# Routed attention and a PReLU feed-forward: the staging loads of the row orderings handed out two scatters later

## The chip, the core and the metric

The kernel runs on one core of a Trainium2 chip. Its engines are TensorE (PE, with weight loads PEld), VectorE (DVE), ScalarE (ACT), GpSimd (POOL) and the queue engine SyncE (SP). The metric is device time in microseconds of one execution. A profile records one execution and takes times from the start of its span.

## The reference

Attention in which a query sees only the keys of its own cluster, then a feed-forward layer with a PReLU. The sizes are 4 batches, 8 heads, 768 tokens, 64 values a head, 16 clusters a head; the layer has 3072 rows, 512 inputs and 2048 hidden values. All in float32.

```python
q_assign = np.argmax(np.einsum('bhsd,hcd->bhsc', q_n, c_n), axis=-1)   # nearest centroid
k_assign = np.argmax(np.einsum('bhsd,hcd->bhsc', k_n, c_n), axis=-1)
mask = q_assign[:, :, :, None] == k_assign[:, :, None, :]
scores = np.where(mask, scale * np.matmul(q, k.transpose(0, 1, 3, 2)), -1000000000.0)
attn = softmax(scores)                                                 # row by row
x = np.matmul(attn, v)              # (B,H,S,D) -> (B*S, H*D)
h = x @ w_in
out = (np.maximum(h, 0.0) + alpha * np.minimum(h, 0.0)) @ w_out
```

## The kernel before, in words

**Pairs and steps.** Two heads of one batch make a pair, numbered 0 to 15. Pairs 0 to 8 compute all scores and mask them. Pairs 9 to 15, seven in all, are first *ordered*: their tokens are sorted by cluster, so that tokens of one cluster lie side by side and only a band of scores need be computed. The program is one long list of steps. A step has five slots; in each slot the host code that writes the program calls pieces of work (`tick`, `prepare`, `feed`) and so fixes the order of the instructions on every engine. Each engine takes its own instructions strictly in that order and waits for others by semaphores. Pieces of the feed-forward layer (L1066, L1084) are fed between the attention's matmuls, so that TensorE always has work.

**One ordering.** `order_rows` (L615) finishes the target row of each token. The rows of q, k and v are then sent through SBUF into a scratch tensor in DRAM in sorted order:

- `order_stage(n, i)` (L654), six loads per ordering, i = 0 to 5. A load is three transfers on SP's queue (q, k and v, L661) into one of two staging buffers, `stage[i % 2]`.
- `order_scatter(n, i, x)` (L666), four scatters per load. Each is one indirect transfer on POOL (L675) that writes 128 rows of the buffer to their places. Before the first of the four, POOL copies the token numbers into the buffer (L672). In front of each slot that has scatters, `pace` (L648) makes POOL wait for a token from ACT, so that scatters spread over time.

The text calls load 2 of ordering 12 "12.2" and its scatters "scatter 12.2". Load i may write its buffer when the four scatters of load i - 2 have landed.

**The list of pieces.** `order_rows` appends all this to the deque `sorting` (L627 to L632), as pairs of a count and a piece: a scatter counts one, a load nothing. In the slots the main loop (L1580 to L1585) takes pieces while there is room; `scatters_at` (L1421) gives 0, 1 or 2 scatters a slot.

**What follows an ordering on SP's queue.** `order_load(n)` (L681), 12 transfers (L688, L697, L706), fetches the sorted rows of pair n from scratch, three or four steps before that pair's scores. DVE transposes them in `order_blocks` (L710, L713). After the pair's attention, `put_back` (L1008) scatters the result rows to their original order with 12 indirect transfers on POOL (L1011), `fetch_back` (L1016) reads them on SP (L1023), and DVE's `turn_back` (L1030) puts them into the layer's input. On the same SP queue are `load` and `load_v` (q, k, v of later pairs, L127 and L141), copies of the weights `w_in_kept` (L1114) and the output stores (L1095, after the `y` of L1092).

Of the kernel before, what the change touches and what calls it, by code (L numbers as in the profile page):

```python
# [23 lines left out]
def kernel(  # L24
# [70 lines left out]
    def later(slots, piece):  # L95
        due.setdefault(now[0] + slots, []).append(piece)
# [277 lines left out]
    NX = GT * NG  # L374
# [114 lines left out]
    PARTS = 3  # L489
    STAGES = 2  # L490
    us, ranks, orders, scratch, sorts = {}, {}, {}, {}, {}
    sorting = deque()
# [112 lines left out]
    def order_ranks(n, ps):  # L605
        member, count = us.pop(n)
        ordp, order = sorts["ordp"], sorts["order"]
        begin = ordp.tile([P, 2], FP32, name="begin")
        nc.vector.tensor_tensor(out=begin, in0=ps[:, 0:2], in1=sorts["shift"], op=ALU.add)
        nc.vector.tensor_copy(out=sorts["begins"][:, n - NO:n - NO + 1], in_=ps[:, 0:1])  # L610
        nc.vector.scalar_tensor_tensor(out=count, in0=count, scalar=begin[:, 1:2],
                                       in1=member, op0=ALU.add, op1=ALU.mult)
        later(1, lambda: order_rows(n, begin, count))

    def order_rows(n, begin, count):  # L615
        ordp, order = sorts["ordp"], sorts["order"]
        by_token = ordp.tile([P, NX, 2, NC], FP32, name="by_token")
        nc.vector.transpose(out=by_token.rearrange("p x h c -> p (x h c)"), in_=count)
        rank = ordp.tile([P, NX, 2], FP32, name="rank")
        nc.vector.tensor_reduce(out=rank, in_=by_token, axis=AX.X, op=ALU.add)  # L620
        off = order.tile([P, NX, 2], I32, name="off")
        nc.vector.tensor_scalar(out=off, in0=rank, scalar1=0.0, scalar2=float(2 * S - 1),
                                op0=ALU.max, op1=ALU.min)
        ranks[n] = off
        whole = tc.dram_tile([2 * 2 * S, P], FP32, name=f"scratch{n}")
        scratch[n] = whole, dram_disjoint_views(whole, 2 * NX)
        for i in range(2 * PARTS + STAGES):  # L627
            if i >= STAGES:
                for x in range(NX // PARTS):
                    sorting.append((1, lambda i=i - STAGES, x=x: order_scatter(n, i, x)))  # L630
            if i < 2 * PARTS:
                sorting.append((0, lambda i=i: order_stage(n, i)))  # L632
        later(2, lambda: order_clusters(n, begin))

    def order_clusters(n, begin):
        ordp, order = sorts["ordp"], sorts["order"]

        begun = ordp.tile([P, HS], BF16, name="mine")
        nc.vector.tensor_scalar(out=begun, in0=sorts["place"], scalar1=begin[:, 0:1],
                                scalar2=None, op0=ALU.is_ge)  # L640
        begunT = asg.tile([P, 2 * NX, NC], BF16, name="top")
        nc.vector.transpose(out=begunT.rearrange("p t c -> p (t c)"), in_=begun)
        first = order.tile([P, 2 * NX], BF16, name="cluster")
        with nc.allow_low_precision(reason="integers up to 16"):
            nc.vector.tensor_reduce(out=first, in_=begunT, axis=AX.X, op=ALU.add)
        firsts[n] = first
# [7 lines left out]
    def order_stage(n, i):  # L654

        b, hp = pairs[n]
        h, part = divmod(i, PARTS)
        head, t = 2 * hp + h, sorts["stage"][i % STAGES]
        rows = slice(part * S // PARTS, (part + 1) * S // PARTS)
        for src, p0, d0 in ((q, 0, 0), (k, TS, 0), (v, TS, D)):  # L660
            nc.sync.dma_start(out=t[p0:p0 + TS, :, d0:d0 + D],  # L661
                              in_=src[b, head, rows].rearrange("(x p) d -> p x d", p=TS))
# [3 lines left out]
    def order_scatter(n, i, x):  # L666
        scattered.setdefault(n, []).append((i, x))
        h, part = divmod(i, PARTS)
        m = NX // PARTS
        xx = part * m + x  # L670
        if x == 0:
            nc.gpsimd.tensor_copy(  # L672
                out=sorts["stage"][i % STAGES].bitcast(I32)[0:TS, :, D],
                in_=sorts["number"][0:TS, part * m:(part + 1) * m])
        nc.gpsimd.indirect_dma_start(  # L675
            out=scratch[n][1][h * NX + xx],
            out_offset=bass.IndirectOffsetOnAxis(ap=ranks[n][:, xx, h:h + 1], axis=0),
            in_=sorts["stage"][i % STAGES][:, x, :], in_offset=None,
            element_offset=h * 2 * S * P)
# [781 lines left out]
    for u in range(-AHEAD, TOGETHER):  # L1461
        for piece in load_at.get(u, []):
            piece()
        n, half, s = steps[max(u, 0)]
# [51 lines left out]
    for u in range(TOGETHER, NS + 1):  # L1516
        for piece in load_at.get(u, []):
            piece()
        if u < NS:
            n, half, s = steps[u]  # L1520
# [50 lines left out]
        for i in slots:  # L1571
# [10 lines left out]
            while sorting and room:  # L1582
                scatters, piece = sorting.popleft()
# [234 lines left out]
```

## Time and profile before

| | us |
|---|---|
| median of 3 runs (951.78 to 957.11) | 953.47 |
| the profiled execution, whole | 932.13 |
| its span, first to last instruction | 930.4 |
| TensorE busy in it | 916.0 |
| VectorE busy | 654.3 |
| GpSimd busy | 389.1 |
| ScalarE busy | 262.2 |

The profile's page gives the busy time of each engine, then the span in forty equal slices (a digit is the busy share in tenths), then the chain of work that ended last, then the costliest groups of instructions. Two more views are used below. The view of waits lists, for one engine, the instruction that stood, what ended its wait, the total time, how often, and the longest. The timeline lists instructions with their start and length, and in brackets the idle time of the engine just before and what ended it. The trace has 168 scatters (L675, mean 1079 ns), 42 loads (126 transfers of 64 KB) and 84 put-backs (L1011, mean 1018 ns). By stretches of the span, TensorE was busy as follows:

| stretch, us | what runs | TensorE busy, us | GpSimd busy, us |
|---|---|---|---|
| 0 to 75 | start, weights arrive | 69.30 | 25.79 |
| 75 to 278 | pairs without an ordering | 202.75 | 32.77 |
| 278 to 477 | orderings 9 to 13, beside pairs without one | 197.57 | 142.21 |
| 477 to 645 | ordered pairs, orderings 13 to 15 beside them | 166.34 | 122.19 |
| 645 to 780 | last ordered pairs | 135.00 | 66.12 |
| 780 to 930 | last part of the layer | 144.99 | 0.00 |

### The profile page before, as it was taken

How to read it: one execution, taken by the hardware profiler on the slowest of the kernel's cores; microseconds unless marked ns; L12 is line 12 of the kernel's file. 1: busy time of each engine (PE TensorE's matmuls, PEld its weight loads, DVE VectorE, ACT ScalarE, POOL GpSimd, SP SyncE). 2: the span in 40 equal slices, each digit the busy share in tenths (PEclk: the TensorE clock that was granted, in tenths of full speed). 3: DMA queues.
4: the chain of work that ended last, by engine and by line, in shares of the span. 5: the costliest groups of instructions: out<-in, count | busy, mean ns of one | idle time of the engine just before them, and what ended most of it. 6: DMA issues, size and time to landing. Idle time of an engine off the chain costs nothing.

```text
span 930.4 us, 11983 instructions
## 1 busy us (share of the span) xinstructions
PE 916.0 (98%) x3963; PEld 494.6 (53%) x3963; DVE 654.3 (70%) x1246; ACT 262.2 (28%) x660; POOL 389.1 (42%) x579
## 2 busy tenths in 40 slices
PE   8999999999999999999999999999999999999997
PEld 5534444445445454455555554555555555556886
DVE  5797788889769699598997899764647135598200
ACT  5764454223123122232222332122222121221000
POOL 2433232200006768587766787677723470000000
PEclk9999999999999999999999999999999999999999
DMA  8433659028001625453762283643511012000000
GB/s 301 132 123 93 148 128 159 18 56 179 26 1 51 153 73 145 88 107 85 156 133 42 50 136 96 142 87 95 97 37 27 12 38 54 1 0 1 23 23 26
DMA packets 226708, 77.71 MB, mean 84 GB/s; under 512 B 210752, under 2 KB 214544, under 8 KB 226640
## 3 DMA queue, kind: packets, MB, share of 16 engines
q1 hardware_dynamic: 217728, 62.72, 30.6%
q0 software_dynamic: 8064, 13.78, 4.7%
q8 instruction: 33, 0.54, 0.3%
q10 hardware_dynamic: 848, 0.39, 0.2%
q14 instruction: 35, 0.29, 0.1%
HBM read 52.25 MB, written 24.25 MB: 82 GB/s over the span
## 4 chain that ended last, share of the span: by engine, by line
PE 94%; DVE 4%; issue 1%; POOL 0%; ACT 0%; DVEq 0%; ACTq 0%; POOLq 0%
PE fps L1066 27%; PE fps L1084 27%; PE sps L784 7%; PE vps L939 7%; PE sps L1302 4%; PE sps L1246 4%; PE fps L784 3%; PE vps L1246 2%; PE vps L1302 2%; PE vps L972 1%; PE mps L972 1%; PE fps L1302 1%; PE fps L1246 1%; PE sps L793 1%; PE mps L894 1%
## 5 line engine op out<-in xcount | busy, mean ns | idle before, releaser
L1066 PE MATMUL fps<-xT,w_in_sb 128*128 128x384 f32 x768 | 259.3, 491 | 0.0
L1084 PE MATMUL fps<-w_out_sb,gT 128*128 128x512 f32 x576 | 254.1, 595 | 0.3 <-DVE gT L1058 0.3
L675 POOL DMA_INDIRECT scratch<-stage,off x168 | 181.3, 1079 | 67.1 <-DMA stage<-in_v_dram 29.5
L1066 PEld LDWEIGHTS fps<-xT,w_in_sb 128*128 128x128 f32 x768 | 142.3, 190 | 103.2 <-issue 4.9
L1084 PEld LDWEIGHTS fps<-w_out_sb,gT 128*128 128x128 f32 x576 | 107.5, 190 | 132.2 <-issue 122.6
L1072 ACT COPY gT<-fps 128x384 f32<-128x384 f32 x96 | 46.0, 479 | 235.9 <-PE fps L1066 235.9
L652 POOL COPY paced<-pace 1x1 f32<-1x1 f32 x204 | 55.0, 270 | 135.7 <-ACT pace L651 135.2
L1058 DVE SCALAR_TENSOR_TENSOR gT<-gT,alpha 128x384 f32<-128x384 f32 x96 | 61.5, 648 | 60.8 <-ACT gT L1072 60.7
L1011 POOL DMA_INDIRECT back<-rows,off x84 | 85.6, 1018 | 22.2 <-issue 16.5
L784 PE MATMUL sps<-qkT 64*128 64x384 f32 (+1 forms) x464 | 85.0, 485 | 0.0
L805 ACT ACTIVATE E<-sps 128x768 f32<-128x768 f32 (+1 forms) x76 | 56.3, 786 | 62.1 <-PE sps L793 39.7
L784 PEld LDWEIGHTS sps<-qkT 64*128 64x128 f32 x464 | 41.2, 186 | 38.6 <-issue 15.5
L825 DVE SCALAR_TENSOR_TENSOR more<-aq,key,more 128x384 f32<-128x384 bf16 (+2 forms) x116 | 60.4, 579 | 0.0
L939 PE MATMUL vps<-E,vt 128*64 128x384 f32 x292 | 54.2, 495 | 1.5 <-DVE xT L1042 1.5
L271 POOL TENSOR_TENSOR w_in_sb<-w_in_sb,power 128x512 f32<-128x512 f32 x16 | 26.9, 1684 | 67.4 <-DVE w_in_sb L268 67.4
L271 POOL TENSOR_TENSOR w_out_sb<-w_out_sb,power 128x512 f32<-128x512 f32 x16 | 22.5, 1411 | 56.0 <-DVE w_out_sb L268 56.0
L825 DVE SCALAR_TENSOR_TENSOR E<-aq,key,E 128x384 f32<-128x384 bf16 (+2 forms) x88 | 45.0, 569 | 0.6 <-ACT E L802 0.6
L835 DVE TENSOR_TENSOR acc<-acc,E 128x768 f32<-128x768 f32 x35 | 33.3, 951 | 14.5 <-ACT E L805 13.6
L907 DVE RECIPROCAL inverses<-mps 64x12 f32<-64x12 f32 (+1 forms) x42 | 10.5, 249 | 45.7 <-PE mps L894 39.8
L1090 ACT COPY y<-fps 128x512 f32<-128x512 f32 x18 | 10.6, 587 | 99.2 <-PE fps L1084 99.2
L1092 DVE TENSOR_TENSOR y<-y,fps 128x512 f32<-128x512 f32 x24 | 16.4, 682 | 27.6 <-PE fps L1084 27.6
L805 ACT ACTIVATE more<-sps 128x768 f32<-128x768 f32 (+1 forms) x40 | 29.2, 764 | 12.2 <-PE sps L784 11.8
(284 smaller groups left out, 1174.1 us busy)
## 6 DMA issues: line engine op xcount, KB each, us to landing
raw<-in_moe_w_in_dram SPq DMA_DIRECT2D x16, 512.0 KB, 5.2
raw<-in_moe_w_out_dram SPq DMA_DIRECT2D x16, 512.0 KB, 4.3
out_dram<-y SPq DMA_DIRECT2D x21, 256.0 KB, 2.4
qk<-scratch SPq DMA_DIRECT2D x56, 96.0 KB, 3.5
qk<-in_q_dram SPq DMA_DIRECT2D x48, 96.0 KB, 3.6
qk<-in_k_dram SPq DMA_DIRECT2D x48, 96.0 KB, 3.6
w_in_kept<-w_in_sb SPq DMA_DIRECT2D x8, 512.0 KB, 3.3
vt<-in_v_dram SPq DMA_DIRECT2D x9, 384.0 KB, 6.5
```

Source lines behind the costliest of these rows:

```text
L652: nc.gpsimd.tensor_copy(out=sorts["paced"], in_=token)
L675: nc.gpsimd.indirect_dma_start(out=scratch[n][1][h * NX + xx], out_offset=bass.IndirectOffsetOnAxis(ap=ranks[n][:, xx, h:h + 1], axis=0), ...
L784: nc.tensor.matmul(out=bank(ps, h, m), lhsT=qkT[r:r + D, S + c * P:S + (c + 1) * P], rhs=qkT[r:r + D, tokens], start=True, stop=not early_ ...
L805: nc.scalar.activation(out=E[:, :, 0:m], in_=ps[:, :, 0:m], func=AF.Exp, scale=SCALE)
L825: nc.vector.scalar_tensor_tensor(out=e, in0=of, scalar=keys[n][:, NJ + c, h:h + 1], in1=e, op0=ALU.is_equal, op1=ALU.mult)
L939: nc.tensor.matmul(out=po[r:r + D, 0:HS], lhsT=vts[n][:, h, c, :], rhs=e[:, h, :], start=(c == 0), stop=(c == NJ - 1))
L1011: nc.gpsimd.indirect_dma_start(out=to[i], out_offset=bass.IndirectOffsetOnAxis(ap=place[:, h, j:j + 1], axis=0), in_=rows[j // HJ][:, j % ...
L1058: nc.vector.scalar_tensor_tensor(out=gs[f], in0=gs[f], scalar=alpha[:, f:f + 1], in1=gs[f], op0=ALU.mult, op1=ALU.max)
L1066: nc.tensor.matmul(out=ps[:, 0:HS], lhsT=w_in_sb[:, c, f * P:(f + 1) * P], rhs=xTs[b, half][:, c, :], start=(c == 0), stop=(c == NCH - 1))
L1084: nc.tensor.matmul(out=ps[:, 0:DM], lhsT=gs[f][:, i * P:(i + 1) * P], rhs=w_out_sb[:, f, :], start=on and f == f0, stop=off and f == f0 + ...
L1246: nc.tensor.matmul(out=bank[to], lhsT=w_in_form(m, x, cc), rhs=rhs[:, cc, :], start=start and cc == 0, stop=cc == KH - 1, skip_group_check ...
L1302: nc.tensor.matmul(out=bank[to], lhsT=g_form(m, x, t), rhs=w_out_form(n, x), start=start and x == 0, stop=x == NQ - 1, skip_group_check=no ...
```

## The change

Before, load i stood in the list directly behind the last of the four scatters that free its buffer (the scatters of load i - 2). After, it stands two scatters further on: between the second and the third scatter of load i - 1, which read the other buffer. The first two loads of an ordering, which come before its first scatter, stay where they were. The last of the held entries is empty. No instruction is added or removed.

```diff
+        held = []
         for i in range(2 * PARTS + STAGES):
-            if i >= STAGES:
-                for x in range(NX // PARTS):
-                    sorting.append((1, lambda i=i - STAGES, x=x: order_scatter(n, i, x)))
-            if i < 2 * PARTS:
-                sorting.append((0, lambda i=i: order_stage(n, i)))
+            stage = [(0, lambda i=i: order_stage(n, i))] * (i < 2 * PARTS)
+            scatters = [(1, lambda i=i - STAGES, x=x: order_scatter(n, i, x))
+                        for x in range(NX // PARTS if i >= STAGES else 0)]
+            if i > STAGES:
+                scatters[2:2] = held.pop()
+            if i < STAGES:
+                sorting.extend(stage)
+            else:
+                held.append(stage)
+            sorting.extend(scatters)
```

`PARTS` is 3, `STAGES` is 2 and `NX // PARTS` is 4. `held` keeps one load until the next four scatters are listed, and then goes in between them.

## The prediction

> **What bounds the kernel now.** I read the busy table and the PE row of the forty slices first, then the chain that ended last, then who waited for whom on PE in the stretch where scatters run (278 to 670 us), and only then SP and POOL, whose queues the change touches.
>
> ```profile
> PE 916.0 (98%) x3963; PEld 494.6 (53%) x3963; DVE 654.3 (70%) x1246; ACT 262.2 (28%) x660; POOL 389.1 (42%) x579
> PE   8999999999999999999999999999999999999997
> PE 94%; DVE 4%; issue 1%; POOL 0%; ACT 0%; DVEq 0%; ACTq 0%; POOLq 0%
> ```
>
> TensorE is busy 916.0 of 930.4 us and carries 94% of the chain. POOL has 0% of it, and DMA does not appear. PE's waits from 278 to 780 us:
>
> ```profile
> PE mps L575 <- issue: 1.4, 1, 1.4
> PE mps L575 <- ACT rows L1005: 0.9, 1, 0.9
> PE fps L784 <- ACT E L802: 0.7, 1, 0.7
> ```
>
> That is all: 3.0 us in three waits, none of them for a transfer. Whatever the change frees on SP or POOL, it can give PE at most these 3.0 us (0.3%) of this execution. The other side is less bounded, so the working below looks for a transfer that comes late. The queues that the change is about do wait (SP, then POOL):
>
> ```profile
> SPq L661 <- DMA scratch<-stage,off: 176.1, 30, 53.0
> POOL scratch L675 <- DMA stage<-in_v_dram: 29.5, 11, 6.1
> ```
>
> SP stands 176.1 us before staging loads until the buffer's scatters have landed; all that is behind it on SP stands too. POOL stands 29.5 us for loads.
>
> **What the change moves.** Nothing is added or removed. Of six loads per ordering, numbers 2 to 5 are handed out later: 7 x 4 = 28 loads, 84 transfers. But SP takes its queue in order and starts a load when the four scatters have landed, not when the program text reaches it. So only what passes a load in SP's own queue can matter. Setting the two instruction streams side by side, PE, DVE, ACT and POOL have the same order; waits differ only in which DMA semaphore they name. On SP 20 of the 28 loads keep their neighbours. Eight are passed (ordering.load):
>
> - 9.4 by a `w_in_kept` store, 9.5 by an output store;
> - 12.4 by an output store; 12.5 by an output store and `order_load(10)`;
> - 13.3 by `fetch_back(9)` and `load(14)`; 13.4 by `load(15)`;
> - 14.3 by an output store and `order_load(13)`;
> - 15.2 by `order_load(14)`.
>
> **Prices.** A load occupies SP 1.93 us (447.96 to 449.89). Where POOL stood for a load, the first scatter began 4.4 to 4.8 us after the load's first issue (459.32 to 463.75, 629.99 to 634.79); I take 4.6. `order_load` occupies SP 7.25 to 8.95 us (450.58 to 457.83; 587.96 to 596.91), an output store 0.4 to 0.6.
>
> *The place with most behind it, 12.4 and 12.5.* SP, then POOL, then DVE in the trace of before:
>
> ```profile
> 444.69 0.60 SPq L661 DMA_DIRECT2D stage<-in_q_dram  x1
> ...
> 447.96 0.61 SPq L661 DMA_DIRECT2D stage<-in_q_dram  x1
> ...
> 450.58 1.10 SPq L688 DMA_DIRECT2D off<-scratch  x2
> 451.73 4.90 SPq L697 DMA_DIRECT2D qk<-scratch  x8
> 456.68 1.15 SPq L706 DMA_DIRECT2D vt<-scratch  x2
> 459.32 0.61 SPq L661 DMA_DIRECT2D stage<-in_q_dram  x1
> ```
>
> ```profile
> 449.31 2.65 POOL L675 DMA_INDIRECT scratch<-stage,off  x1 [2.62 <-DMA stage<-in_v_dram]
> ...
> 456.63 0.98 POOL L675 DMA_INDIRECT scratch<-stage,off  x1 [0.28 <-POOL stage L672]
> ...
> 481.52 1.35 POOL L675 DMA_INDIRECT scratch<-stage,off  x1 [6.06 <-DMA stage<-in_v_dram]
> ```
>
> ```profile
> 458.22 0.97 DVE L713 STREAM_TRANSPOSE qkT<-qk 128x768 f32<-128x768 f32 x1
> ...
> 459.68 0.98 DVE L713 STREAM_TRANSPOSE qkT<-qk 128x768 f32<-128x768 f32 x1
> ...
> 511.43 1.04 DVE L1030 STREAM_TRANSPOSE xT<-qk 128x384 f32<-128x384 f32 x2 [2.69 <-DMA qk<-back]
> ...
> 515.36 0.62 DVE L907 RECIPROCAL inverses<-mps 64x24 f32<-64x24 f32 x2 [2.43 <-PE mps L894]
> ```
>
> The reader is to see 12.4 and 12.5 on SP in front of `order_load(10)` (L688, L697, L706), two scatters of POOL that follow them, and the DVE transposes L713 that consume what `order_load(10)` fetched, with no wait, though the last of its eight `qk` transfers left SP at 456.6.
>
> After: the output store goes at 444.6 (its `y` was ready at 434.7), 12.4 at 445.1: scatter 12.4 at 449.8, +0.5. The second store and `order_load(10)` run 447.2 to 455.1, 2.8 us earlier; 12.5 goes at 455.2 instead of 447.96, and its first scatter at 459.8 instead of 456.63: **POOL +3.1**. Behind it in turn: 13.1 waits for these scatters, 463.3 becomes 466.4; `order_load(11)` behind that on SP 465.93 becomes 469.0; 13.2 475.9 becomes 479.0; its scatter 481.52 becomes 484.6; the put-backs of pair 9 behind it on POOL begin at 486.3 instead of 483.2. Cover: `order_load(11)` issues its last `qk` transfer at 476.7 (issue to landing 3.5) and the transposes want it at 485.3, so about 5 us remain. Among pair 9's put-backs POOL stands 0.79 + 0.44 + 1.60 + 0.56 = 3.4 us for the pace tokens and its own issue, so the last one (504.37) and `fetch_back(9)` (506.87) keep their time. **Sum on PE: 0.**
>
> *14.3.* The store's `y` is ready at 573.3, so `order_load(13)` goes at 581.9 instead of 587.96. 14.3 goes at 590.9 instead of 585.36, its scatter at 595.5 instead of 590.29: POOL +5.2. But the next load, 14.4, then goes at 593.0 instead of 597.09, and the 5.83 us that POOL stood for it fall away: scatter 14.4 at 601.1 against 601.58. Given back within one buffer; sum 0.
>
> *15.2.* `order_load(14)` at 615.2 instead of 620.52; 15.2 at 624.1, scatter 628.7 against 627.92; POOL stood 1.61 us at the next buffer, which takes it. Sum 0.
>
> *The rest.* 13.3 goes at about 514 instead of 478.65, but its scatter runs at 537.0; 13.4 at 549.2, its scatter at 557.7; 9.4 and 9.5 still leave when their scatters land (302.9 and 310.5), since the stores that pass fit into SP's idle time (9.65 and 4.97 us). Sum 0.
>
> *What comes earlier.* `order_load` 10, 13 and 14 by 2.8 to 6.1 us. For 10, the last `qk` transfer began at 455.87; with 3.5 us to landing that is 459.4, against the transpose at 459.68: 0.3 us to spare. For 13 it is 598.5 against 599.67. DVE did not wait, so this gains nothing in this execution; it widens two thin margins. Its worth lies between 0 and the 3.0 us that PE waits; I take 0, because none of the three waits names these transposes.
>
> **A rule against the change.** The Trainium skill, "Trainium Kernel Development and Optimization", section Best Practices, says to double-buffer so that transfers overlap compute. Read strictly, the hand-out belongs at the freeing scatter: with two of four scatters gone (1.31 us apart, 463.75 to 465.06), 2 x 1.31 = 2.6 us remain for a load of 4.6, POOL would stand 2.0 us each, 28 x 2.0 = 56 us. The trace says otherwise: SP idles until landing anyway, so 20 loads start as before, and the eight others cost POOL 3.1 + 5.2 + 0.8 us, all given back. The same skill, "DMA: Bandwidth & Descriptors", section on the anatomy of one DMA, puts any semaphore wait on the issuing sequencer; that agrees with the 176.1 us row. I follow the row.
>
> **Sum.** The profiled execution took 932.13 us, 1.7 around a span of 930.4; the change adds 0, so 932.1. The timed runs have median 953.47, 21.3 us more, which no view here explains; I put the difference 0 on the median: **953.5**.
>
> **Rivals.**
> 1. *Slower: POOL's delay is not absorbed at pair 9's put-backs.* Place: load 12.5 behind `order_load(10)`. Price: its whole delay, 455.2 - 447.96 = 7.2 us, reaches `fetch_back(9)`; DVE stands for it (2.69 us already at L1030) and has 2.43 us of its own wait to PE before the masks are late: 7.2 - 2.4 = +4.8, 958.3. It decides from 2.4 us at `fetch_back(9)` on. For it: DVE already waits there. Against: 3.1, not 7.2, reaches POOL, and 3.4 us of pauses lie between.
> 2. *Faster: the thin margins of `order_load` 10 and 13 are missed in the timed runs*, inside the 21.3 us. They get 2.8 and 6.1 us earlier: at most -8.9, 944.6; by this trace, at most -3.0.
> 3. *Nothing measurable, with PE's small waits shifting* by up to 3.0 us either way: 950.5 to 956.5. This is the forecast's own range.
>
> **How the numbers follow.** About 0.5% (4.8 us) is what a measurement of this kernel can tell from no change. Forecast with case 3: 0.80. Rival 1: 0.12. Rival 2: 0.08. The range goes beyond 950.5 to 956.5 by part of both rivals and the spread of the runs shown (951.8 to 957.1): 948.5 to 959.
>
> **What would show it.** SP: L688 first issued near 447.8, 581.9 and 615.2 for orderings 10, 13, 14. POOL: a new wait of about 3 us at 12.5 and 5 at 14.3, the one of 5.83 at 14.4 gone; L1023 of pair 9 still near 506.9. PE: waits from 278 to 780 us still about 3 us. Wrong if PE's waits grow by more than 5 us, or if DVE's wait at L1030 passes 5 us.

## The result and the profile after

| | before | after |
|---|---|---|
| median of 22 timed runs each, same chip, us | 953.15 (946.92 to 960.67) | 958.69 (951.55 to 965.08) |
| ratio of the runs | | 1.0056, 95% interval 1.0035 to 1.0076 |
| span of the profiled execution, us | 930.4 | 955.5 |

The change makes the kernel 0.56% slower, about 5.3 us. The profiles must not be subtracted: the first profile of before was taken in an execution of 932 us, and no timed run of before in this comparison was under 946.92. The new profile is an ordinary one, so most of its 25 us over the old one is not the change. Two slow timed runs further below, one of before at 1589.9 us and one of e3 at 970.5, are left out of all ratios and averages.

In the code after, lines behind L632 stand six lower than before (L675 is now L681). First the page's lines for TensorE (busy time, slices of the span, granted clock, chain) in the profile after:

```profile
PE 924.0 (97%) x3963; PEld 498.5 (52%) x3963; DVE 656.6 (69%) x1246; ACT 263.5 (28%) x660; POOL 386.0 (40%) x579
PE   8999999999999999999789999999799999999997
PEclk9999999999999999999989999999899999999999
PE 83%; DVE 9%; another core or an unknown queue 2%; issue 2%; ACT 1%; SPq 1%; DMA 1%; POOL 0%; ACTq 0%; DVEq 0%; POOLq 0%
```

Two slices of TensorE fall to 7, and with each, or just behind it, a slice of the clock falls to 8. Those two places are new against the page of before, where TensorE's row has nothing but nines between its first and last digits and the clock's row nothing but nines. The longest waits of PE between 200 and 800 us, and those of SP and POOL for staging over the whole span (engine, line, releaser, us in total, times, longest):

```profile
PE fps L1072 <- ACT more L808: 7.9, 1, 7.9
PE fps L790 <- ACT gT L1078: 5.5, 2, 4.9
PE mps L978 <- DVE inverses L913: 1.7, 2, 1.0
```

```profile
SPq L667 <- DMA scratch<-stage,off: 89.7, 20, 14.2
...
POOL scratch L681 <- DMA stage<-in_v_dram: 31.4, 9, 7.6
```

PE's 3.0 us of waits have become 19.7 (these rows and six smaller ones), 13.4 of them in the first two rows. SP stands 86 us less before staging loads, as the change would have it, and nothing became faster for it. Then the place with most behind it. On SP load 12.5 now stands behind `order_load(10)` (L694, L703, L712):

```profile
449.91 1.11 SPq L694 DMA_DIRECT2D off<-scratch  x2
451.06 4.91 SPq L703 DMA_DIRECT2D qk<-scratch  x8
456.02 1.40 SPq L712 DMA_DIRECT2D vt<-scratch  x2
457.59 0.61 SPq L667 DMA_DIRECT2D stage<-in_q_dram  x1
```

POOL's scatters that stood for a load, in the timeline of after (start, us, instruction, idle before and releaser):

```profile
451.75 1.17 POOL L681 DMA_INDIRECT scratch<-stage,off  x1 [4.57 <-DMA stage<-in_v_dram]
...
462.30 0.98 POOL L681 DMA_INDIRECT scratch<-stage,off  x1 [4.37 <-DMA stage<-in_v_dram]
...
486.68 1.02 POOL L681 DMA_INDIRECT scratch<-stage,off  x1 [7.57 <-DMA stage<-in_v_dram]
```

These are 12.4, 12.5 and 13.2. The wait of 4.37 us at 12.5 is the one that the prediction expected, at about 3. And the windows around the first new hole, with one from the second as the last row (busy us and instructions of each engine, granted clock, busy share of the DMA engines, GB/s):

```profile
460.00:470.00 10.00, 8.97 (x52) 5.37 (x52) 9.88 (x17) 3.20 (x9) 6.64 (x11) 1.00 0.24 65
470.00:477.40 7.40, 2.47 (x22) 1.38 (x18) 3.08 (x7) 0.00 (x0) 6.47 (x11) 1.00 0.88 170
477.40:484.20 6.80, 3.82 (x6) 2.16 (x7) 2.18 (x5) 1.91 (x4) 1.54 (x5) 0.50 1.04 202
484.20:500.00 15.80, 15.80 (x60) 8.52 (x59) 14.07 (x26) 3.80 (x14) 7.47 (x13) 1.00 0.07 19
...
671.00:675.40 4.40, 0.80 (x2) 0.29 (x2) 0.62 (x1) 0.80 (x4) 3.19 (x5) 1.00 0.14 45
```

The first columns behind the length are PE, PEld, DVE, ACT and POOL. From 470 to 477.4 us PE does 2.47 us of work, ACT none, and POOL alone works on through most of it. Then comes a window of 6.8 us at half the clock; PE stands for its first 3.0 us and works through the other 3.8. The Trainium skill's page "TensorE: Matmul & The Clock Gate", Part 1, says that the clock goes to half after at least one idle window of about 3.4 us. This stop fits that: the clock falls 4.9 us after the last matmul's modelled end (472.5). The profile of e1 below does not show it: there the clock falls at 476.1 with no gap over 0.87 us between the matmuls before. Either way a stop with such a window behind it costs twice, as standing time and as slow work.

### The profile page after: what moved, and what is told of

It is laid out like the page before. It is cut to its first block, busy times and chain, and to the rows that moved or that the text cites. A ratio compares the mean times of both kernels' runs of the same rounds, so it can differ in the third digit from the quotient of the medians.

```text
span 955.5 us, 11982 instructions
## 1 busy us (share of the span) xinstructions
PE 924.0 (97%) x3963; PEld 498.5 (52%) x3963; DVE 656.6 (69%) x1246; ACT 263.5 (28%) x660; POOL 386.0 (40%) x579
## 4 chain that ended last, share of the span: by engine, by line
PE 83%; DVE 9%; another core or an unknown queue 2%; issue 2%; ACT 1%; SPq 1%; DMA 1%; POOL 0%; ACTq 0%; DVEq 0%; POOLq 0%
PE fps L1090 24%; PE fps L1072 23%; PE sps L790 6%; PE vps L945 6%; PE sps L1308 4%; PE sps L1252 4%; PE fps L790 2%; PE vps L1252 2%; PE vps L1308 2%; PE fps L1308 1%; PE fps L1252 1%; PE vps L978 1%; PE mps L978 1%; DVE acc L841 1%
## 5 line engine op out<-in xcount | busy, mean ns | idle before, releaser
L681 POOL DMA_INDIRECT scratch<-stage,off x168 | 178.2, 1061 | 70.4 <-issue 32.9
L1017 POOL DMA_INDIRECT back<-rows,off x84 | 88.0, 1048 | 23.1 <-issue 18.3
L271 POOL TENSOR_TENSOR w_in_sb<-w_in_sb,power 128x512 f32<-128x512 f32 x16 | 23.7, 1482 | 70.1 <-DVE w_in_sb L268 70.1
L790 PE MATMUL fps<-qkT 64*128 64x384 f32 (+1 forms) x136 | 31.1, 494 | 7.1 <-ACT gT L1078 5.5
```

The lines of the kernel that those rows point to most:

```text
L681: nc.gpsimd.indirect_dma_start(out=scratch[n][1][h * NX + xx], out_offset=bass.IndirectOffsetOnAxis(ap=ranks[n][:, xx, h:h + 1], axis=0), ...
L790: nc.tensor.matmul(out=bank(ps, h, m), lhsT=qkT[r:r + D, S + c * P:S + (c + 1) * P], rhs=qkT[r:r + D, tokens], start=True, stop=not early_ ...
L1017: nc.gpsimd.indirect_dma_start(out=to[i], out_offset=bass.IndirectOffsetOnAxis(ap=place[:, h, j:j + 1], axis=0), in_=rows[j // HJ][:, j % ...
```

## What the stops are, and what they are not

A *stop* is here a place where TensorE stands although the trace shows no unmet need. The program order of PE is the same in all these kernels, so the start of every matmul can be compared with the start of the same one in the first profile; the difference is the lag, and a stop shows as a jump of the lag. In after the lag goes from 2.0 to 13.1 us between 465 and 485 us of the first profile's time, and from 16.1 to 25.1 between 650 and 670. The rest comes in steps of a few us.

PE's timeline of the first profile and of after at the same work (start, us, instruction, idle before and releaser), first before:

```profile
467.46 0.81 PE L784 MATMUL fps<-qkT 64*128 64x320 f32 x4
468.10 1.19 PE L784 MATMUL sps<-qkT 64*128 64x384 f32 x8
469.22 2.85 PE L1066 MATMUL fps<-xT,w_in_sb 128*128 128x384 f32 x8
```

then after:

```profile
470.64 0.81 PE L790 MATMUL fps<-qkT 64*128 64x320 f32 x4
471.28 1.19 PE L790 MATMUL sps<-qkT 64*128 64x384 f32 x8
480.38 4.12 PE L1072 MATMUL fps<-xT,w_in_sb 128*128 128x384 f32 x6 [7.91 <-ACT more L808]
```

The releaser "ACT more" is not the cause. ACT itself stood 11.9 us for these scores (`ACT more L808 <- remote: 11.9, 1, 11.9`): PE started them at 471 us, their ends are modelled as 472.5, but the semaphore that reports them done rose only at 479.9 to 480.0 (in the first profile within 0.05 us of the modelled end). So PE waits for ACT, ACT for PE's own work, and that work is reported 7.6 to 8.5 us late. Nothing that the trace shows holds it. It is not the DMA load alone: in the other stop of after (the last row of the windows above) the DMA engines are 0.14 busy, and PE does 0.80 of 4.4 us.

## The experiments

All were timed against before on the same chip. The experiments fell on different chips: before took 960.0 us on the chip of e1 to e4 and 958.9 on that of e5 to e8, with stops in every profile taken there; it took 933.3 and 932.6 on that of e9 to e12, at two times,, where no profile shows a stop.

**e1: before again.** No edit. It asks whether the first profile stands for the timed runs.

> The kernel before, once more, timed against itself and profiled on the same chip as the next three. Both theories expect a ratio of 1.000, and its spread is the floor for the other ratios. Its profile tells whether the profile of before (930.4 us, clock 1.000) is typical. Theory A (the passes on SP delay POOL and then DVE): a typical before has a full clock and a span near 950. Theory B (stops of TensorE, each followed by a window at half clock, decide the time, and an arrangement changes how many there are): a typical before also has such windows, clock about 0.992 to 0.995, two windows of 6.8 us.

Ratio 0.9991 (0.9961 to 1.0022), span 957.6 us, clock 0.991. In the page of this profile the rows of PE and of its clock:

```profile
PE   8999999999999999999999999799899999999997
PEclk9999999999999999999999999999899999999999
```

Before has the holes too, and windows at half clock at 476.1, 605.9 and 677.5 us. They account for the 21.3 us between the first profile and the timed runs: this profile is 27 us behind the first one. Why the first profile has no stops is not on record, but its 932.13 us lie within what before takes on the chip of e9 to e12 (931.88 to 935.35) and outside all other timed runs of before (946.92 and more). So it may well come from another chip than the timed runs, and stand for every execution there.

**e2: only ordering 12 moved; e3: all but ordering 12.** The change's lines, kept for one ordering or for the other six:

```diff
-            if i > STAGES:
-                scatters[2:2] = held.pop()
...
+            at = 2 if n == 12 else 0          # e3: 0 if n == 12 else 2
+            if i > STAGES and at:
+                scatters[at:at] = held.pop()
...
             sorting.extend(scatters)
+            if not at and i >= STAGES:
+                sorting.extend(stage)
```

> Only ordering 12 has its loads handed out two scatters later; the other six stand as before. Theory A, with its place at load 12.5 behind order_load(10): the whole difference of the change, ratio 1.005 to 1.006, and POOL stands about 4 us before scatter 12.5. Theory B: between 1.000 and 1.003, since no single pass carries it.

> All orderings but 12 have their loads two scatters later. Theory A: ratio 1.000 to 1.001, POOL does not stand before scatter 12.5. Theory B: 1.003 to 1.006.

e2: 1.0038 (1.0021 to 1.0055). e3: 1.0000 (0.9981 to 1.0019). What cost can be told from nothing sits in ordering 12, though the moves in the other six are 24 of 28. Among these is 14.3, where POOL also came late, by the same kind of passing.

**e4: all loads handed out four scatters later.** The lines of e2 and e3 with `at = 4` for every ordering.

> All seven orderings, and each load handed out four scatters later, directly before the scatters that read it, instead of two. Theory A: 12.5 still goes behind order_load(10), and more loads are passed, so the ratio is at least that of the change, 1.006 to 1.015. Theory B: any ratio from 1.000 to 1.010, not growing with the distance; the number of half-clock windows follows the time.

1.0072 (1.0045 to 1.0100), not told apart from the change itself (1.0056). 12.5 stands behind `order_load(10)` in both, which fits a cost that does not grow with the distance; but SP's order in e4's trace has 10.3, 11.5 and 12.3 passed as well, so e4 is no clean test of that.

**e5: only load 12.5 moved; e6: all but 12.5.**

```diff
-            if i > STAGES:
-                scatters[2:2] = held.pop()
-            if i < STAGES:
-                sorting.extend(stage)
-            else:
-                held.append(stage)
+            scatters[2:2] = held
+            held = stage if i >= STAGES and ((n, i) == (12, 5)) else []     # e6: !=
             sorting.extend(scatters)
+            sorting.extend([] if held else stage)
```

> Before, with one of the 28 moves alone: load 12.5, handed out two scatters later, so that it stands behind order_load(10) on SP. Theory A (the cost sits at this load: its first scatter about 4 us later on POOL, then 13.1 and order_load(11)): ratio 1.003 to 1.005, all of what ordering 12 cost (1.0038). Theory B (the cost is spread: TensorE's stops and half-clock windows fall a little longer with any change in the pattern of transfers): 1.000 to 1.002.

> The change without that one move: all loads two scatters later, 12.5 where it was. Theory A: 0.998 to 1.002. Theory B: 1.003 to 1.006, as the whole change (1.0056).

e6: 0.9996 (0.9970 to 1.0022): without this one move of 28 no cost can be measured. e5: 1.0017 (0.9996 to 1.0038), which holds both nothing and all of e2's 1.0038. So the move of 12.5 is needed for the cost; that it is enough is not shown. 12.4 may add its part: in after it went behind an output store that took 2.0 us on SP, and POOL stood 4.57 us for it.

**e7: POOL late, with SP's order untouched.**

```diff
-        if x == 0:
+        for _ in range(17 if (n, i, x) == (12, 5, 0) else x == 0):
             nc.gpsimd.tensor_copy(
```

> Before with SP's order untouched, and sixteen more POOL copies of 0.26 us each (the copy of token numbers into the staging buffer, repeated) ahead of the first scatter of 12.5: POOL is 4.2 us late there. Theory A1 (what costs is that POOL is late): 1.003 to 1.005. Theory A2 (what costs is SP's order, order_load(10) earlier and 12.5 behind it): 0.999 to 1.001. Theory B: 0.999 to 1.002.

1.0051 (1.0030 to 1.0072). POOL's timeline around 12.5 in this run:

```profile
458.41 5.49 POOL L672 COPY stage<-number 64x4 int32<-64x4 int32 x17
464.50 0.98 POOL L675 DMA_INDIRECT scratch<-stage,off  x1 [0.61 <-DMA stage<-in_q_dram]
```

Nothing passes anything on SP here. The scatter of 12.5 is 464.50 - 458.18 = 6.3 us later than in e1, 4.4 of it more than PE's own lag (5.7 against 3.8 us at that point), and the cost is as large as the change's. So a delay of these scatters, and of what stands behind them, is enough for such a cost without `order_load(10)` being early. How the cost follows the delay is not shown: in e5 the same scatter is 3.4 us later, counted in the same way, and the ratio is 1.0017. The sixteen copies are themselves a second difference, and no run has them without the delay. PE's timeline of this run also shows a stop from its beginning:

```profile
475.02 0.99 PE L784 MATMUL sps<-qkT 64*128 64x384 f32 x5
476.18 0.35 PE L784 MATMUL sps<-qkT 64*128 64x224 f32 x1 [0.16 <-issue]
476.92 0.35 PE L784 MATMUL sps<-qkT 64*128 64x224 f32 x1 [0.39 <-issue]
478.34 0.35 PE L784 MATMUL sps<-qkT 64*128 64x224 f32 x1 [1.08 <-issue]
482.65 1.65 PE L1066 MATMUL fps<-xT,w_in_sb 128*128 128x384 f32 x2 [3.96 <-ACT more L802]
```

The eight matmuls that took 1.19 us in the first profile start further and further apart, with nothing waited for ("issue"), until PE stands.

**e8: `order_load` in three parts.** The second half of q and k leaves three slots later, v six.

```diff
         for w in range(2):
+            later(3 * w, lambda w=w: load_qk(n, whole, w)) if w else load_qk(n, whole, w)
+        later(6, lambda: load_sorted_v(n, whole))
...
```

> Before, with each order_load cut in three: row numbers and first half of q and k as before, the second half three slots later, v six slots later. Nothing is computed otherwise. Theory A: no change, 0.999 to 1.001, since nothing waits for v or the second half in these slots. Theory B, if it is the burst of an order_load that makes TensorE's stop at 470 us long: 0.990 to 0.997, with a shorter stop there.

1.0001 (0.9982 to 1.0019), the stop near 470 us is there as before. A shorter burst of this kind does not help.

**The lag in the profiles with stops.** Each line is one profile; columns are the jump of the lag between 465 and 485 us, all of it at 720 us, and the timed ratio:

```text
load 12.5 on time            jump   lag    ratio     load 12.5 late             jump   lag    ratio
e1 before again               7.0   27.3   0.9991    after                      11.1   25.1   1.0056
e3 all but ordering 12        5.4   27.8   1.0000    e2 only ordering 12         9.3   28.8   1.0038
e6 all but 12.5               4.4   31.3   0.9996    e4 four scatters later      8.8   37.2   1.0072
e8 order_load in parts        6.7   31.9   1.0001    e5 only 12.5                7.7   32.6   1.0017
                                                     e7 POOL late               10.2   30.8   1.0051
```

The two groups, of four and five profiles, do not overlap in the first column: 5.9 us on average with 12.5 on time, 9.4 with it late, 3.5 us more. That is the size of e2's cost (0.38% of 960 is 3.6 us). But the lag at the end, 29.6 against 30.9 us on average, does not separate them, and after has the smallest of all: single executions differ by more than the effect, and other stops are shorter where this one is long. The timed runs can be asked too, since each has its mean granted clock. The difference from before on the same chip, averaged over all of them (standard error of each 0.0005 to 0.0007):

```text
e1 +0.0001   e3 +0.0007   e6 +0.0001   e8 -0.0002       e5 -0.0006   e2 -0.0016   e7 -0.0019   e4 -0.0049
```

The three versions that are clearly slower are the three with a clearly lower clock, so they do spend more time in half-clock windows. A clock lower by 0.001 is 0.96 us lost of 960: by this estimate 1.5 of e2's 3.6 us and 1.8 of e7's 4.9 us are slow work, and the rest has to be standing or waiting. So more or longer stops are the best account of the cost. That it is the stop near 470 us rests on the nine profiles alone, and is not shown to be all of it.

**e9: `order_load(11)` late by itself.** In these profiles the jump follows the start of `order_load(11)`, counted on PE's own time (the lag at 465 us taken off): it began at 462.8 to 463.7 in e1, e3 and e6, and at 466.2 to 469.5 in the five with 12.5 late (e4 among them, where the scatter of 12.5 itself is only 1.3 us later than in the first profile). It waits on SP behind load 13.1, which waits for the scatters of 12.5. To move it alone, its first two transfers were made three times over:

```diff
-        for h in range(2):
+        for h in [0, 1] * (3 if n == 11 else 1):
             r0 = 2 * h * S
```

> Before, with the two transfers of row numbers that begin order_load(11) made three times over (the same rows to the same place): its q, k and v leave SP some 2 to 5 us later, with POOL's scatters up to 13.1 on time. Theory L (it is order_load(11) starting later that lengthens TensorE's stop near 470 us, as the profiles so far suggest: it began 462.8 to 463.7 us on TensorE's own clock of work with stops of 4.4 to 7.0 us, and 466.2 to 469.5 with stops of 7.7 to 11.1): ratio 1.002 to 1.005. Theory P (it is POOL's scatters of 12.5 to 13.1 being late): 0.999 to 1.001.

**e10: load 13.1 handed out behind `order_load(11)`, else before; e11 and e12: the same on top of the whole change.**

```diff
+                    if (n, i, x) == (13, STAGES, 3):
+                        sorting.append((0, lambda: order_stage(n, 1)))
                     sorting.append((1, lambda i=i - STAGES, x=x: order_scatter(n, i, x)))
-            if i < 2 * PARTS:
+            if i < 2 * PARTS and (n, i) != (13, 1):
```

> Before, with load 13.1 handed out behind order_load(11) and not ahead of it: order_load(11) starts some 2 us earlier, the scatters of 13.1 some 7 us later. Theory L: 0.996 to 1.000, the stop near 470 us 5 us or shorter. Theory P: 1.004 to 1.009.

> The whole change, with load 13.1 handed out behind order_load(11): 12.5 is as late as in the change, order_load(11) starts some 5 us earlier than there. Theory L: 0.998 to 1.002, what the change cost is given back. Theory P: 1.005 to 1.010.

> The same kernel as the run before (the whole change, load 13.1 behind order_load(11)), since that chip ran the kernel before in 933 us, and TensorE made no stops on it. If before takes some 955 to 960 us again: Theory L (order_load(11) starting late lengthens the stop near 470 us) says 0.998 to 1.002; Theory P (the scatters of 12.5 to 13.1 being late) says 1.005 to 1.010. If before takes some 933 us, both say 0.999 to 1.001.

These ran where there are no stops; theories L and P of the expectations are that the late `order_load(11)` lengthens the stop, and that the late scatters do. e9: 1.0003 (0.9995 to 1.0012). e10: 1.0001 (0.9993 to 1.0010). e11: 0.9996 (0.9988 to 1.0005). e12: 1.0001 (0.9992 to 1.0009). They can't tell the two theories apart, because what both would lengthen was absent; which of the late transfers it is stays open. They show something else. The waits of POOL for loads in e11 between 440 and 490 us, and then those of PE between 200 and 800 (lines there are up to ten higher than in before):

```profile
POOL scratch L685 <- DMA stage<-in_v_dram: 13.8, 3, 5.1
```

```profile
PE mps L575 <- issue: 1.4, 1, 1.4
PE mps L575 <- ACT rows L1015: 0.9, 1, 0.9
PE fps L794 <- ACT E L812: 0.7, 1, 0.7
```

POOL stands 13.8 us for three loads, 5.11 of them at 12.5 (scatter at 462.17), and PE has the three waits of the first profile to the tenth. In e10 scatter 13.1 is at 477.58 instead of 469.74, nearly 8 us late, in e9 the q and k of `order_load(11)` leave at 474.75 instead of 467.15, and neither can be measured. Where TensorE does not stop, the slack is as large as the trace of before said. The change by itself, without the move of 13.1, was not run on such a chip.

No version here beats before.

## Why the prediction was partly right

The range held (958.69 in 948.5 to 959), by 0.3 us and by luck: its upper end had been widened for a rival whose mechanism proved false. The likeliest value, 953.5, was 5.2 us low, and a cost of this size had been given 0.12. The mechanism was right as far as the engines' waits go, and wrong in that nothing but these waits was reckoned to reach TensorE.

- **What the change moves.** Right: SP's order in the two traces differs by exactly the eight loads named. The prices are right too, once PE's lag at that point is taken off (a rough correction: in e1 this scatter on POOL is 1.5 us behind the first profile, PE 3.8). At 12.5, POOL's scatter is at 462.30 - 1.9 = 460.4 (predicted 459.8); `order_load(10)` at 449.91 - 1.9 = 448.0 (447.8); `order_load(11)` at 471.49 - 2.0 = 469.5 (469.0). Mis-sized in this group are POOL's waits at 12.5 and 14.3, 4.37 and 6.83 us instead of about 3 and 5; the one at 14.4 is gone, as predicted (0.28 us of issue).
- **Absorbed among pair 9's put-backs.** Right. SP's `fetch_back(9)` in after, then DVE's wait for it:

```profile
519.94 2.03 SPq L1029 DMA_DIRECT2D qk<-back  x4
```

```profile
525.14 1.04 DVE L1036 STREAM_TRANSPOSE xT<-qk 128x384 f32<-128x384 f32 x2 [3.33 <-DMA qk<-back]
```

  519.94 less the lag of 13.1 is 506.8, predicted 506.9. DVE waits 3.33 us, below the 5 us named as the sign of failure; as worded, for all of L1030, that sign could not tell anything, since before itself has a wait of 6.6 us there, later on.
- **Rival 1** gave 958.3, almost the measured time, and is false all the same: its place, `fetch_back(9)`, is not late. It named the right load and the wrong way from there to TensorE.
- **Rival 2** (thin margins of `order_load` 10 and 13, up to 8.9 us) fell. Both came earlier as expected, 10 in e2 and 13 in e3, and no gain shows: e2 is slower and e3 the same.
- **The rule of double-buffering**, 56 us by the prediction's strict reading of it against 0 by the row: the row was much nearer, and the rule had the sign. Six of seven orderings cost nothing measurable (e3).
- **The step that failed** is the sum: "which no view here explains; I put the difference 0 on the median". The 21.3 us were TensorE's stops, which the first profile doesn't have and all nine profiles of 955 us and more have. What the change does among them was put at 0 without a reason; the change measured +5.3 us, its ordering 12 alone 3.6 (e2), and a delay of POOL alone 4.9 (e7). That this term is near 0 where there are no stops is what e11 and e12 suggest (0.9996 and 1.0001, the change with load 13.1 handed out later). The sign of failure "PE's waits grow by more than 5 us" did come in after (3.0 to 19.7), but e1, before itself, has 18.9 us of them: the growth is not the change's.

## What to carry to other kernels

When the profiled execution is 2% away from the timed runs, get a second profile, on the chip of the timed runs, before pricing anything: here the difference was stops that the first trace doesn't show, and slack read from that trace held only where there are none. A delay that a trace says is absorbed can still cost where TensorE is stopping anyway (here about 0.4 to 0.5%); test it by putting the same delay in by itself, as e7 does, rather than by tracing the waits. And compare two profiles by the start of the same instruction: a jump of the lag shows where time went when the waits of several engines point at each other.

## What was not expected of the hardware

- The same kernel took 933 us on one chip and 953 to 960 on others. The difference is the stops, 27 us in e1 against at most 1.9 us of lag in e9 to e12. Why TensorE stops is open. Each chip was met at one time or within minutes, so not even that it is the chip, and not the time, is shown. The stops come again near the same work (near 470, between 560 and 630 and near 670 us of the first profile's time, in most of the nine profiles), with the DMA engines 0.88 busy at one and 0.14 at another, and a shorter burst (e8) doesn't remove them.
- A stop shows first as matmuls that start further and further apart with "issue" as the releaser (0.16, 0.39, 1.08 us in e7) and as semaphores that rise long after the modelled end (7.6 to 8.5 us in after). A window at half clock, 3.4 to 10.2 us long, goes with most of them; the stop of e6 near 470 us, 4.4 us of lag, has none.
- Idle copies on POOL that delay it by 4.4 us cost 0.51% of the kernel's time (e7), though POOL is busy for only 42% of the span and has 0% of the chain in the page of before.
